# Linear attention with a rational feed-forward block on one core: scaling constants in three tasks, the last output products in another order, and a new instruction order

## The chip, the core and the metric

The kernel runs on one core of a Trainium2 chip. The metric is the device time of one execution in microseconds (us): of three runs before the change the median is 539.79 (539.32 to 540.35). The engines are TensorE (PE in the profile, its weight loads PEld), VectorE (DVE), ScalarE (ACT), GpSimd (POOL) and SyncE (SP), which issues all DMAs here.

## The reference

For each of 4 x 8 heads, a linear attention with decay runs over 768 steps of 48 values; its output, 3072 tokens of 384 values, goes through a feed-forward block whose function is a quotient of two polynomials:

```python
for t in range(S):
    kt, vt, rt = (k[:, :, t], v[:, :, t], r[:, :, t])
    cur = np.einsum('bhd,bhe->bhde', u[None] * kt, vt)
    y[:, :, t] = np.einsum('bhd,bhde->bhe', rt, state + cur)
    state = w[None, :, :, None] * state + np.einsum('bhd,bhe->bhde', kt, vt)
...
h = x @ w_in
P = a[0] + a[1] * h + a[2] * h2 + a[3] * h3
Q = 1.0 + np.abs(b[0]) * np.abs(h) + np.abs(b[1]) * h2
g = P / (Q + 1e-06)
return (g @ w_out).astype(np.float32)
```

w_in is 384 x 2048, w_out 2048 x 384; all is 32-bit float.

## The kernel before

*Attention.* Tokens are worked in 24 blocks of 128, two blocks a pair, 12 pairs. r and k are scaled by powers of the decay, which the start makes (wcol clamps the decays, cen is their power, pw and pk hold powers and inverses, wrn and wkn the same turned); each block is turned on TensorE (tr, tk, L517), and a pair then has products kv (L566), a (L545), and y in two parts (L595: from the state, then its own). VectorE evicts a through a mask (av, L553); vo is a copy of half of v at other partitions (made by att_v with a copy or a DMA), read by the second part of y. The bonus term is r times k (m, L498), times ub (L503), summed to dt (L508) and times v (L512). y is added to m (L611), and m is turned into x (L623), kept as a high part xth and a low part xtl (L637).

*Feed-forward.* 12 tiles of 256 tokens; the 2048 columns are cut in slots of 2 x 128 (the very last slot is cut in two of 128). Per slot: f1 makes h with three products per piece (high by high, low by high, high by low; L648), or, for the first tile, one with the full weights (L654). Ten instructions on ScalarE, VectorE and GpSimd make g of h: z, q, t, ln, exp on ScalarE (L701 to L721), u3, hi, p, d on VectorE (L725 to L741), lo mostly on GpSimd (L745). Then f2 adds to the output o, half a tile (hf) at a time, again three products per 128 columns (L658 to L660). When a tile's columns are all in, put_out evicts each half with the scale SG (L792 on ScalarE, L794 on VectorE, L787 where a partial sum is added), and put_dma sends it (L799).

*Weights* come as pieces of 32-bit words (sto of w_out, 384 KB; sti of w_in, 512 KB; L378), and are made into wfo and wfi (L401), a high part whio or whii (L424) and a low part wloo or wloi (L421).

*Constants of the slots' functions.* pro_beta (L263 to L274) takes absolute values of the coefficients on ScalarE, floors two of them on VectorE (ctmp, L268), takes ln and exp of half of it on ScalarE (root), and sets four constants on VectorE (L271 to L274), two of them in the PSUM tile in which ScalarE also writes (sqs). pro_squares (from L281) refines the root and makes the other constants. The q and t of every slot wait for it.

*Order.* Nothing is scheduled while the program is built: build() and prologue() list about 2200 tasks with their engines, dependencies and buffers, and the text ORDER names the tasks by number in the order in which placed() issues them, a letter choosing the engine (D, A, G) where there is a choice. "w3" stands for three fillers: products of zeros on TensorE (L980 into a tile of its own, L978 into an open output, to which they add nothing), 60 in all. Each engine works its own instructions in this order and waits by semaphores.

```python
        for n_, e in order:
            if n_ != "warm":
                fns[n_](ENG.get(e))
            elif began:
                nc.tensor.matmul(grown, wzero, wones, start=False, stop=False)
            else:
                nc.tensor.matmul(warm[:, 0:DM], wzero, wones, start=True, stop=True)
```

## Time and profile before

| | us |
|---|---|
| median of three runs (lowest, highest) | 539.79 (539.32, 540.35) |
| the profiled execution: its time | 540.16 |
| its span | 538.4 |
| busy in the span: TensorE | 518.8 (96%) |
| VectorE | 429.7 (80%) |
| ScalarE | 398.6 (74%) |
| GpSimd | 255.0 (47%) |

The profile is one execution; its times count from the start of the span. Its page gives busy times, the chain of work that ended last, and groups of instructions by line. The trace behind it answers questions on a stretch: the busy time of each engine in it, what an engine waited for, the instructions in order of time. L12 is line 12 of the kernel before; a duration is the busy time of an instruction, and "idle before <- X" is the time that its engine sat idle ahead of it and who ended that.

### The profile page before, as it was taken

The numbers are of one execution on the slowest core, as the hardware profiler recorded it, in microseconds if no ns is written. First come the engines' busy times: TensorE is split into PE (matmuls) and PEld (weight loads), VectorE is DVE, ScalarE is ACT, GpSimd is POOL, SyncE is SP. The second block draws the span as 40 slices with busy tenths as digits, with TensorE's granted clock in tenths as the row PEclk, the third lists the DMA queues.
The fourth block names the chain that finished last, engine by engine and source line by source line (L and its number), as shares of the span: only waits on it lengthen the run. The fifth ranks groups of instructions, "written<-read, shape, count | busy, mean of one in ns | idle before, by whom it ended". The sixth has DMA issues, their size and how long they took to land.

```text
span 538.4 us, 14858 instructions
## 1 busy us (share of the span) xinstructions
PE 518.8 (96%) x6111; PEld 492.5 (91%) x6111; DVE 429.7 (80%) x716; ACT 398.6 (74%) x648; POOL 255.0 (47%) x244
## 2 busy tenths in 40 slices
PE   7779999999999999999999999999999999999995
PEld 3558898899999999999999999999999999999994
DVE  5899998999889786786887787787886777686681
ACT  5889989997856669684787656777666767888791
POOL 2588981644554655635255444256444422233231
PEclk9999999999999999999999999999999999999998
DMA  8977454830004304023250023140030000000001
GB/s 177 281 180 184 129 128 138 177 68 1 1 17 89 84 19 72 1 61 66 40 118 1 2 61 80 33 86 6 16 75 2 15 18 1 2 29 1 31 1 35
DMA packets 91661, 34.07 MB, mean 63 GB/s; under 512 B 84929, under 2 KB 88002, under 8 KB 91586
## 3 DMA queue, kind: packets, MB, share of 16 engines
q1 hardware_dynamic: 91586, 33.05, 26.7%
q8 instruction: 50, 0.82, 0.6%
q14 instruction: 25, 0.20, 0.1%
HBM read 28.32 MB, written 4.72 MB: 61 GB/s over the span
## 4 chain that ended last, share of the span: by engine, by line
PE 84%; DVE 8%; ACT 3%; DMA 2%; issue 1%; SPq 0%; DVEq 0%; ACTq 0%
PE h L648 33%; PE o L658 12%; PE o L659 12%; PE o L660 12%; PE y L595 5%; PE a L545 2%; PE kv L566 2%; PE h L654 2%; DMA sto<-in_moe_w_out_dram 2%; PE tr L517 2%; PE tk L517 1%; PE x L623 1%; DVE q L735 1%; DVE g L731 1%; DVE pk L322 1%
## 5 line engine op out<-in xcount | busy, mean ns | idle before, releaser
L745 POOL TENSOR_TENSOR g<-q,z 128x512 fp32r<-128x512 f32 (+1 forms) x97 | 125.7, 1295 | 214.9 <-DVE q L741 126.7
L648 PE MATMUL h<-xth,whii 128*128 128x256 f32 x528 | 152.0, 288 | 2.0 <-DVE q L735 1.7
L648 PE MATMUL h<-xtl,whii 128*128 128x256 f32 x528 | 148.1, 280 | 0.0
L648 PE MATMUL h<-xth,wloi 128*128 128x256 f32 x528 | 148.0, 280 | 0.0
L658 PE MATMUL o<-whio,g 128*128 128x384 f32 x384 | 134.3, 350 | 0.0
L660 PE MATMUL o<-whio,g 128*128 128x384 f32 x384 | 130.0, 339 | 0.0
L659 PE MATMUL o<-wloo,g 128*128 128x384 f32 x384 | 130.0, 338 | 0.0
L648 PEld LDWEIGHTS h<-xth,whii 128*128 128x128 f32 x528 | 99.4, 188 | 4.5 <-DVE q L735 2.7
L648 PEld LDWEIGHTS h<-xtl,whii 128*128 128x128 f32 x528 | 99.5, 188 | 0.0
L648 PEld LDWEIGHTS h<-xth,wloi 128*128 128x128 f32 x528 | 99.5, 188 | 0.0
L707 ACT ACTIVATE w<-q,off,root 128x512 f32<-128x512 f32 (+1 forms) x97 | 75.3, 779 | 29.9 <-DVE q L735 15.9
L731 DVE SCALAR_TENSOR_TENSOR g<-h,sig,z 128x512 fp32r<-128x512 f32 (+1 forms) x97 | 72.0, 742 | 30.2 <-ACT z L721 26.5
L712 ACT ACTIVATE t<-h,off,root 128x512 f32<-128x512 f32 (+1 forms) x97 | 73.4, 767 | 24.1 <-PE h L648 21.6
L701 ACT ACTIVATE q<-h 128x512 f32<-128x512 f32 (+1 forms) x97 | 56.3, 587 | 37.6 <-PE h L648 36.0
L725 DVE SCALAR_TENSOR_TENSOR h<-t,sig,h 128x512 f32<-128x512 f32 (+1 forms) x97 | 71.7, 742 | 15.5 <-ACT t L712 12.3
L735 DVE SCALAR_TENSOR_TENSOR q<-w,sig,g 128x512 f32<-128x512 f32 (+1 forms) x97 | 72.1, 743 | 6.5
L741 DVE SCALAR_TENSOR_TENSOR q<-h,sig,q 128x512 f32<-128x512 f32 (+1 forms) x97 | 72.1, 744 | 2.7
L658 PEld LDWEIGHTS o<-whio,g 128*128 128x128 f32 x384 | 72.1, 188 | 1.1
L660 PEld LDWEIGHTS o<-whio,g 128*128 128x128 f32 x384 | 72.1, 188 | 0.5 <-POOL g L745 0.5
L659 PEld LDWEIGHTS o<-wloo,g 128*128 128x128 f32 x384 | 72.2, 188 | 0.0
L717 ACT ACTIVATE z<-w,lnb 128x512 f32<-128x512 f32 (+1 forms) x97 | 65.9, 679 | 8.4 <-POOL g L745 3.4
L721 ACT ACTIVATE z<-z,lnb 128x512 f32<-128x512 f32 (+1 forms) x97 | 69.7, 718 | 2.1
(144 smaller groups left out, 669.5 us busy)
## 6 DMA issues: line engine op xcount, KB each, us to landing
sto<-in_moe_w_out_dram SPq DMA_DIRECT2D x16, 384.0 KB, 4.0
sti<-in_moe_w_in_dram SPq DMA_DIRECT2D x12, 512.0 KB, 5.0
rh<-in_r_dram SPq DMA_DIRECT2D x24, 192.0 KB, 4.0
kh<-in_k_dram SPq DMA_DIRECT2D x24, 192.0 KB, 3.8
vn<-in_v_dram SPq DMA_DIRECT2D x24, 192.0 KB, 4.1
out_dram<-os SPq DMA_DIRECT2D x24, 192.0 KB, 2.6
vo<-in_v_dram SPq DMA_DIRECT2D x16, 96.0 KB, 3.8
wraw<-in_w_dram SPq DMA_DIRECT2D x1, 1.0 KB, 2.6
```

Source lines behind the costliest of these rows:

```text
L648: nc.tensor.matmul(o, w_[nm][:, c], x_[:, cc], start=(n == 0), stop=(n == 3 * NCC - 1))
L658: nc.tensor.matmul(o, hi, w_["hi"], start=first, stop=False)
L659: nc.tensor.matmul(o, hi, w_["lo"], start=False, stop=False)
L660: nc.tensor.matmul(o, lo, w_["hi"], start=False, stop=last)
L707: nc.scalar.activation(g["w"], w_, AF.Square, scale=RB, bias=KB)
L712: nc.scalar.activation(g["t"], g["h"], AF.Square, scale=RA, bias=KA)
L721: nc.scalar.activation(g["z"], g["z"], AF.Exp, scale=-1.0, bias=lnb[:, 1:2])
L725: nc.vector.scalar_tensor_tensor(g["h"], g["t"], KAP, g["h"], op0=ALU.add, op1=ALU.mult)
L731: nc.vector.scalar_tensor_tensor(g["hi"], g["h"], c0, g["z"], op0=ALU.add, op1=ALU.mult)
L735: nc.vector.scalar_tensor_tensor(g["q"], g.get("w", g["q"]), qe, g["hi"].bitcast(F32), op0=ALU.add, op1=ALU.mult)
L741: nc.vector.scalar_tensor_tensor(g["d"], g["h"], c0, g["q"], op0=ALU.add, op1=ALU.subtract)
L745: e.tensor_mul(g["lo"], g["d"], g["z"])
```

## The change

*Constants.* pro_beta becomes three tasks, which ORDER can place apart: the absolute values (ScalarE), the floor (VectorE), ln and exp (ScalarE). The four constants are set in pro_load, at the start; two of them get a tile of their own, pts, and pro_squares reads them there.

*The last output products.* The last two slots hold one piece of 128 columns each, with two half tiles hf: before, their f2 ran in the order (first slot, half 0), (first, 1), (last, 0), (last, 1); now (first, 0), (last, 0), (first, 1), (last, 1). The last eviction, of half 1, is cut in two of 192 columns: put_out does one on ScalarE, the new task put_rest the other on VectorE, and the DMA waits for the second.

*Order.* ORDER is a new text, with other places, engines and fillers (66) for the whole program.

```diff
 ORDER = """
-0 58 59 35 12 13 14 16 15 w1 60 61 62 17 18 20 234 156 157 w1 3 51 52 1 7 w15 243 w1 22 23 w3 10 233 236G 241 25 19 158 159 53
...
+236 158 247 0 1 60 6 37 14 3 7 4 w1 15 16 17 18 20 22 19 w16 29 159 160 161 162 163A 21 23 38 61 62 63 235 238G w2 12 13 248
...
+        tab["sq"] = ps_o.tile([P, 512], F32, tag="o0", name="sqs")
+        tab["pts"] = cst.tile([P, 2], F32, name="pts")
+        nc.vector.memset(tab["pts"][:, 0:1], 0.5)
+        nc.vector.memset(tab["pts"][:, 1:2], 1.0)
+        nc.vector.memset(lnb[:, 0:1], QC * 2.0 ** -LN_SHIFT)
+        nc.vector.memset(lnb[:, 1:2], -LN_SHIFT * math.log(2.0))
...
     def pro_beta():
         nc.scalar.activation(beta[:, 0:2], coef[:, 4:6], AF.Abs)
         nc.scalar.activation(cabs, coef, AF.Abs)
-        tab["sq"] = ps_o.tile([P, 512], F32, tag="o0", name="sqs")
-        half, pts = tab["sq"][:, 0:2], tab["sq"][:, 4:6]
+
+    def pro_floor():
         nc.vector.tensor_scalar(rx, cabs[:, 3:6:2], SMALL, None, op0=ALU.max)
+
+    def pro_root():
+        half = tab["sq"][:, 0:2]
         nc.scalar.activation(half, rx, AF.Ln)
         nc.scalar.activation(root, half, AF.Exp, scale=0.5)
-        nc.vector.memset(pts[:, 0:1], 0.5)
-        nc.vector.memset(pts[:, 1:2], 1.0)
-        nc.vector.memset(lnb[:, 0:1], QC * 2.0 ** -LN_SHIFT)
-        nc.vector.memset(lnb[:, 1:2], -LN_SHIFT * math.log(2.0))
...
-        half, raw, pts = (tab["sq"][:, x : x + 2] for x in (0, 2, 4))
+        half, raw, pts = tab["sq"][:, 0:2], tab["sq"][:, 2:4], tab["pts"]
...
+    EH = DM // 2
...
-        if e is nc.scalar:
+        if s == NS - 1 and hf:
+            nc.scalar.activation(os_[:, 0:EH], o_[:, 0:EH], AF.Copy, scale=SG)
+        elif e is nc.scalar:
             e.activation(os_, o_, AF.Copy, scale=SG)
...
+    def put_rest():
+        nc.vector.tensor_scalar(oss[NTILE - 1, 1][:, EH:DM], ops[NTILE - 1][1][:, EH:DM], SG, None, op0=ALU.mult)
...
+                if s >= NS - 2 and s + hf != NS - 2:
+                    prev = {(NS - 1, 0): ("f2", NS - 2, 0), (NS - 2, 1): ("f2", NS - 1, 0), (NS - 1, 1): ("f2", NS - 2, 1)}[s, hf]
...
+                    if end:
+                        add(("or",), lambda e: put_rest(), "D", [("os", s, hf)], use=[("o", so), buf])
...
-        add(("sq",), lambda e: pro_squares(), "D", [("beta",)])
+        add(("floor",), lambda e: pro_floor(), "D", [("beta",)])
+        add(("root",), lambda e: pro_root(), "A", [("floor",)])
+        add(("sq",), lambda e: pro_squares(), "D", [("root",)])
```

What stands where now, engine by engine. (Numbers at the end of a name tell buffers apart; the lines of the new kernel lie 5 to 12 further down.) First SyncE's issues at the start of the program, before and now:

```order
L236 DMA wraw<-in_w_dram 64x4x1
L237 DMA wraw<-in_w_dram 48x4x1
L378 DMA sto_129<-in_moe_w_out_dram 128x768
L467 DMA rh_101<-in_r_dram 128x8x48
L378 DMA sto_152<-in_moe_w_out_dram 128x768
L378 DMA sti_2_159<-in_moe_w_in_dram 128x1024
L261 DMA ur<-in_u_dram 1x384
L467 DMA kh_102<-in_k_dram 128x8x48
```

```order
L472 DMA rh_101<-in_r_dram 128x8x48
L383 DMA sto_117<-in_moe_w_out_dram 128x768
L472 DMA kh_104<-in_k_dram 128x8x48
L236 DMA wraw<-in_w_dram 64x4x1
L237 DMA wraw<-in_w_dram 48x4x1
L267 DMA ur<-in_u_dram 1x384
L383 DMA sto_141<-in_moe_w_out_dram 128x768
L472 DMA kh_102<-in_k_dram 128x8x48
L472 DMA rh_103<-in_r_dram 128x8x48
```

wraw (the decays) and ur stood first and seventh; now r, a piece of w_out and a k stand ahead of wraw.

Next VectorE's queue around the floor (ctmp), before and now:

```order
L424 CAST whii_2_230<-wfi_2_215 128x512
L490 TENSOR_TENSOR kh_102<-kh_102,wkn 128x8x48
L268 TENSOR_SCALAR ctmp<-cabs 128x2
L271 MEMSET sqs 128x1
L272 MEMSET sqs 128x1
L273 MEMSET lnb 128x1
L274 MEMSET lnb 128x1
L523 TENSOR_TENSOR kt<-tk_197,pk 112x512
L523 TENSOR_TENSOR kt<-tk_236,pk 112x512
```

```order
L406 SCALAR_TENSOR_TENSOR wfi_1_385<-cp_380,upi_1_382 128x512
L616 TENSOR_TENSOR m_200<-y_0_348,m_200 128x4x48
L616 TENSOR_TENSOR m_208<-y_0_348,m_208 128x4x48
L274 TENSOR_SCALAR ctmp<-cabs 128x2
L616 TENSOR_TENSOR m_200<-y_1_349,m_200 128x4x48
L429 CAST whii_1_447<-wfi_1_385 128x512
L616 TENSOR_TENSOR m_208<-y_1_349,m_208 128x4x48
L429 COPY xth_450<-x_439 128x3x128
L406 SCALAR_TENSOR_TENSOR wfi_0_456<-cp_389,upi_0_391 128x512
L406 SCALAR_TENSOR_TENSOR wfi_0_466<-cp_445,upi_0_453 128x512
L286 RECIPROCAL sqs<-root 128x2
```

The floor moved from ahead of the turned k and r (kt, rt) to among the additions of y to m; its reader on VectorE, the first instruction of pro_squares (the reciprocal), follows some way behind it, and the memsets are gone from here.

Then VectorE's queue shortly ahead of the first second-tile products (L648), at the masks av of the second pair, before and now:

```order
L577 TENSOR_TENSOR st_110<-kv_1_612,st_110 112x384
L553 TENSOR_TENSOR av<-a_0_670,mask 128x512
L725 SCALAR_TENSOR_TENSOR h_491<-t_591,sig,h_491 128x512
L401 SCALAR_TENSOR_TENSOR wfo_761<-cp_660,upo_664 128x384
L553 TENSOR_TENSOR av<-a_1_671,mask 128x512
L731 SCALAR_TENSOR_TENSOR g_821<-h_491,sig,z_758 128x512
L735 SCALAR_TENSOR_TENSOR q_651<-w_653,sig,g_821 128x512
L611 TENSOR_TENSOR m_463<-y_0_726,m_463 128x4x48
L611 TENSOR_TENSOR m_550<-y_0_726,m_550 128x4x48
L611 TENSOR_TENSOR m_463<-y_1_727,m_463 128x4x48
L741 SCALAR_TENSOR_TENSOR q_651<-h_491,sig,q_651 128x512
```

```order
L406 SCALAR_TENSOR_TENSOR wfi_1_612<-cp_585,upi_1_591 128x512
L429 COPY kt<-tk_607 112x512
L429 CAST whii_1_619<-wfi_1_612 128x512
L429 COPY st_110<-kv_0_630 112x384
L730 SCALAR_TENSOR_TENSOR h_527<-t_615,sig,h_527 128x512
L582 TENSOR_TENSOR st_110<-kv_1_631,st_110 112x384
L558 TENSOR_TENSOR av<-a_0_673,mask 128x512
L406 SCALAR_TENSOR_TENSOR wfo_709<-cp_626,upo_665 128x384
L429 COPY vo_112<-vn_580 64x192
L429 COPY vo_112<-vn_587 64x192
L558 TENSOR_TENSOR av<-a_1_674,mask 128x512
L736 SCALAR_TENSOR_TENSOR g_814<-h_527,sig,z_715 128x512
```

Two copies of vo and a cast whii now stand among the functions of the second slot (u3 at L725, now L730; hi at L731, now L736); these copies and casts stood on ScalarE.

Last the end of the program, with the semaphores that each instruction waits for: the last evictions on ScalarE before, on VectorE now (ScalarE's half, L799, waits for PE_49 alone among the engines).

```order
L721 ACTIVATE z_7484<-z_7484,lnb 128x256 [waits Activation_49]
L717 ACTIVATE z_7491<-w_7440,lnb 128x256 [waits Pool_49]
L721 ACTIVATE z_7491<-z_7491,lnb 128x256 [waits Activation_49]
L792 ACTIVATE os_0_7509<-o_0_7259,sig 128x384 [waits DMAHW5_49,PE_49]
L792 ACTIVATE os_1_7514<-o_1_7260,sig 128x384 [waits DMAHW6_49,DMAHW4_49,PE_49]
```

```order
L736 SCALAR_TENSOR_TENSOR g_7512<-h_7426,sig,z_7508 128x256 [waits DVE_49,PE_49,Activation_49]
L740 SCALAR_TENSOR_TENSOR q_7485<-w_7504,sig,g_7512 128x256 [waits DVE_49,Pool_49]
L746 SCALAR_TENSOR_TENSOR q_7485<-h_7426,sig,q_7485 128x256 [waits DVE_49]
L803 TENSOR_SCALAR os_0_7523<-o_0_7283,sig 128x384 [waits DMAHW4_49,PE_49]
L807 TENSOR_SCALAR os_1_7530<-o_1_7284,sig 128x192 [waits DMAHW5_49,DMAHW2_49,Activation_49]
```

VectorE now evicts half 0 (L803), and its half of half 1 (L807) waits for Activation_49, ScalarE's semaphore, at the count that ScalarE's half (L799) brings it to. On SyncE the output DMA of an early tile, whose data have long been there, now stands between the last two output DMAs.

More of the change, by code (lines that the diff above doesn't have):

```diff
@@ new lines @@
+1092 1040D 1046 1048 1049 1050 1051 1026 1063 1052 1053 1054G 1028 1062 1064 1065 1066 211 212A 1075 1076 1077 1067 1068 1069
+213D 1070G 1041 393G 1042 1055 1057 1056 1058 1078 1080 1079 1081 1082 1083 1093 1095 1098 1084D 1094 1096 1097 1099 401 403
+1071 1072 1105 1106 1107 1109 234G 1085 1086 379 380G 402 404 1088 408 1123 1087 435G 438G 436G 1100 1101 409 415 410 414 1102
+1108 1110 1111 1112 1113 1114 1089 1124 1127 1125 411 412A 413 1126 1137 1138 1139 1128 1115 1130 416 417D 418 1103 1104 420
@@ new lines @@
+1312 1344 1346 1347 510 511A 512 1349 1350 1358 1360 1361 1325 1326 1339 1340 1351 562 560 515 541 540A 561 563G 622 534G 565G
+566D 1359 1362 573 546 547 525A 539A 542 1369 1370 1363 544 1364 543 545 1352 1353 549 520 1365 521D 551 1371 1372 1374 1375
+1373 1376 556 1377 1378 1379 1387 1388 1389 1390 1391 1394 1366 1354 1367 1392 575 574 576G 577D 579D 1393 550 1401 1402 1403
+571 572A 1405 1395 1396 1397 1415 1416 1368 564G 569 1380 1381 1404 1406 1407 570A 578D 584 585A 1408 1409 1410 1398 1411 1412
@@ L127 @@
+2104 2105 2106 2107 2108 2112 2115 2125 2113 2114 2116 2080 2126 2139 2117 2081D 2082 2079 2140 2118 2127 2128 2130 2129 2095
[3 rows of a table added]
+2199 2201 2202 2203 2204 2205 2193 2206D 2207 1090 2208 2209 2210 2211
 """
@@ L931, in build @@
                     prv = [("os", max(s_ for s_ in range(s) if SL[s_][0] == f and closes(s_)), hf)] if some else []
-                    add(("os", s, hf), lambda e, s=s, hf=hf: put_out(s, hf, e), "D" if some else "AD", [("f2", s, hf), *prv],
+                    end = s == NS - 1 and hf == 1
+                    add(("os", s, hf), lambda e, s=s, hf=hf: put_out(s, hf, e), "A" if end else "D" if some else "AD", [("f2", s, hf), *prv],
                         new=[] if some else [(spare(s), buf)], use=[("o", so)] + ([buf] if some else []))
+                    if end:
+                        add(("or",), lambda e: put_rest(), "D", [("os", s, hf)], use=[("o", so), buf])
                     if done:
-                        add(("od", f, hf), lambda e, f=f, hf=hf: put_dma(f, hf), "S", [("os", s, hf)], use=[buf] + keep * (s == NS - 1))
+                        add(("od", f, hf), lambda e, f=f, hf=hf: put_dma(f, hf), "S", [("or",) if end else ("os", s, hf)], use=[buf] + keep * (s == NS - 1))
     def prologue():
```

139 lines of the change are left out of this document (65 added, 74 removed), and 13 rows, old and new, of the table ORDER.

## The prediction

> **What bounds the kernel now.** I read the page, then the busy time in three stretches, the fillers, the waits and the end. The first row is the page's busy time; the stretches give for each engine its busy time and count, then TensorE's granted clock, the DMA share and GB/s.
>
> ```profile
> PE 518.8 (96%) x6111; PEld 492.5 (91%) x6111; DVE 429.7 (80%) x716; ACT 398.6 (74%) x648; POOL 255.0 (47%) x244
> core 0: us, PE busy (x) PEld busy (x) DVE busy (x) ACT busy (x) POOL busy (x), PEclk, DMA share, GB/s
> 0.00:52.40 52.40, 41.57 (x674) 30.00 (x674) 42.67 (x94) 41.43 (x82) 33.41 (x47) 1.00 0.86 204
> 52.40:60.00 7.60, 7.36 (x174) 6.58 (x171) 7.35 (x14) 7.13 (x13) 5.48 (x6) 1.00 0.83 223
> 60.00:532.00 472.00, 469.91 (x5272) 455.91 (x5271) 379.71 (x610) 349.79 (x554) 216.12 (x191) 1.00 0.20 45
> L980 PE MATMUL warm<-wones,wzero 128*128 128x384 bf16 x45 | 12.2, 402 | 2.3 <-POOL wzero L245 2.3
> L978 PE MATMUL o<-wones,wzero 128*128 128x384 bf16 x10 | 2.5, 327 | 0.0
> 52.40 0.38 PE L648 MATMUL h<-xth,whii 128*128 128x256 f32 x1
> ```
>
> TensorE (PE) bounds the kernel from 52.40 us, where the first h product by two-part weights (L648) starts. From 60 us on it is busy 469.91 of 472.00, and 0.30 of the rest lies behind its last product (the eviction that waits for it starts at 531.70, below). So between 52.40 and the tail only 0.24 + 1.79 = 2.0 us are idle. Before 52.40 it is busy for 41.57 of 52.40, and 55 of the 60 fillers (products with zeros) stand there too. At the granted clock 1.00 everywhere, the time is therefore: when the first L648 product starts, plus a nearly solid stream of products, plus the tail. The products are the same before and after; what stands ahead of the first L648 product is the same set as well (three kv, two a and y groups, 12 products of L654, 12 of L658 to L660). So the change can win only the idle time of the start, the 2.0 us, or the tail.
>
> In the start VectorE (DVE) sets the pace: 42.67 busy of 52.40, idle mainly before its first result and in the waits of the next rows (time waited, how often, the longest). The last rows are what it does just before 52.40.
>
> ```profile
> DVE pw L315 <- ACT cen L309: 2.8, 1, 2.8
> DVE av L553 <- PE y L595: 1.0, 2, 0.8
> DVE av L553 <- PE a L545: 0.9, 1, 0.9
> 51.38 0.56 DVE L637 TENSOR_TENSOR xtl<-x,xth 128x384 fp32r<-128x384 f32 x1
> 51.85 0.68 DVE L424 COPY kt<-tk 112x512 f32<-112x512 f32 x1
> ```
>
> The product at 52.40 needs the second low half of x (L637), which ends at 51.94. Rows that follow each other without waiting start 0.08 sooner than the last one ends (51.38 + 0.56 against 51.85).
>
> The tail: end of the chain, the last evictions and output DMAs, the time from issue to landing of each of the two (the last row of each DMA answer), and the two slices of 1 us before the last landing.
>
> ```profile
> 531.70 0.58 ACT os L792
> 531.78 0.87 SPq L799 DMA_DIRECT2D out_dram<-os  x2
> out_dram<-os SPq DMA_DIRECT2D x1, 192.0 KB, 1.9
> out_dram<-os SPq DMA_DIRECT2D x1, 192.0 KB, 4.1
> 534.00:535.00 1.00, 0.00 (x0) 0.00 (x0) 0.00 (x0) 0.00 (x0) 0.00 (x0) 0.50 0.04 9
> 535.00:536.00 1.00, 0.00 (x0) 0.00 (x0) 0.00 (x0) 0.00 (x0) 0.00 (x0) 0.50 0.06 12
> q8 instruction: 50, 0.82, 0.6%
> ```
>
> The two DMAs of equal size start some 0.5 apart, yet one lands after 1.9 and the other after 4.1. In between, at 9 and 12 GB/s, only stragglers move. q8 carries instructions in pieces of 0.82 MB / 50 = 16 KB.
>
> **The change part by part.** (1) *Constants.* ScalarE (ACT) computes |b| and |a,b|, VectorE floors (ctmp), ScalarE takes ln and exp, VectorE sets constants. Before, all of it is one task:
>
> ```profile
> 14.86 1.07 DVE L268 TENSOR_SCALAR ctmp<-cabs 128x2 f32<-128x2 f32 x1
> 14.39 1.42 POOL L490 TENSOR_TENSOR kh<-kh,wkn 128x384 f32<-128x384 f32 x1 [0.28 <-ACT beta L264]
> 15.96 0.18 ACT L269 ACTIVATE sqs<-ctmp 128x2 f32<-128x2 f32 x1 [1.47 <-DVE ctmp L268]
> 16.41 0.06 DVE L271 MEMSET sqs<- 128x1 f32 x1 [0.48 <-ACT root L270]
> ```
>
> The floor, of 128x2, takes 1.07 and ends 0.12 after GpSimd's (POOL) kh product, at 15.81; then VectorE idles 0.48 for the root, since its memsets write the tile in which ScalarE works. From 14.86 to the first memset, at 16.41, 1.55 pass for a floor that alone takes about as long as wcol's 0.17 (next fence). Now the four memsets (0.06 each) stand at the program's start, where VectorE waits 2.68 for wcol, and other instructions stand between the floor and its reader. Gain on VectorE 1.55 - 0.17 + 0.1 for the memsets: -1.5; bounds -0.6 (the floor again waits 0.9 for GpSimd) and -1.6. ScalarE's 1.47 of waiting goes too; it isn't the pace here.
>
> (2) *Start.* The decays (wraw) are now issued behind the first r, a weight piece and the first k, not first. The next rows show a small transfer behind large ones, and ScalarE's first steps.
>
> ```profile
> 4.30 0.34 SPq L261 DMA_DIRECT2D ur<-in_u_dram  x1
> 9.88 0.91 PE L298 MATMUL us<-ur,ones 1*128 1x384 f32 x2 [0.56 <-DMA ur<-in_u_dram]
> 3.73 0.17 DVE L305 TENSOR_SCALAR wcol<-wraw 112x4 f32<-112x4 f32 x1 [2.68 <-DMA wraw<-in_w_dram]
> 5.75 0.52 ACT L396 ACTIVATE cp<-sto 128x384 f32<-128x384 f32 x1 [3.66 <-DMA sto<-in_moe_w_out_dram]
> 6.42 0.20 ACT L309 ACTIVATE cen<-sq 112x4 f32<-112x4 f32 x1
> ```
>
> ur, 1.5 KB issued at 4.30, is there at 9.88, 5.6 later: a small transfer lands behind the large ones issued before it. Ahead of wraw now stand 192 + 384 + 192 KB, 0.79 MB, which at the first stretch's 204 GB/s take 3.9. So wraw is there between 3.73 and 7.6; I take 6.4, nearer to the late end as ur is. Before, cen stands on ScalarE behind the weight piece (5.75) and ends at 6.62; now it is first there, and ends three steps of 0.2 behind wraw, at 7.1. Cost +0.5; bounds -2.3 and +1.6.
>
> (3) *Work moved to VectorE.* In its queue up to the second L637 (rows 3 to 91 before, 7 to 96 after) the new order has more: one PSUM copy of 512 (0.68, the row at 51.85), two casts whii (0.41 unhindered), one whio (0.35), two products of SBUF tiles (as L498, 0.55: by ub, and v by dt), four copies of vo (0.25). It has less: one wfo (0.54), one kh scaling (as L498) and two xth (0.55 each). The rows (min/median/max ns for three, then mean):
>
> ```profile
> L424 DVE COPY vo<-vn x4: 254/804/1375, 229.3 to 361.9; 64x192 f32<-64x192 f32 x4
> L424 DVE CAST whio<-wfo x11: 348/350/1419, 30.7 to 103.3; 128x384 fp32r<-128x384 f32 x11
> L424 DVE CAST whii<-wfi x6: 414/416/1366, 14.1 to 101.7; 128x512 fp32r<-128x512 f32 x6
> L424 DVE CAST whio<-wfo 128x384 fp32r<-128x384 f32 x11 | 6.7, 624 | 0.1
> L401 DVE SCALAR_TENSOR_TENSOR wfo<-cp,upo 128x384 int32<-128x384 int32 x15 | 8.2, 544 | 0.3 <-ACT upo L387 0.2
> L498 DVE TENSOR_TENSOR m<-rh,kh 128x384 f32<-128x384 f32 x1 | 0.6, 552 | 0.0
> L424 DVE CAST xth<-x 128x384 fp32r<-128x384 f32 x4 | 2.2, 546 | 0.0
> ```
>
> More: 0.68 + 0.82 + 0.35 + 1.10 + 1.00 = 3.95; less: 0.54 + 0.55 + 1.10 = 2.19; that is 1.76, and for six more instructions 6 x 0.08 of overlap off: +1.3.
>
> (4) *Waits for GpSimd.* Seven of these (whii, whio, vo) read and write SBUF only, and such instructions wait:
>
> ```profile
> 34.45 2.50 POOL L421 TENSOR_TENSOR wloi<-wfi,whii 128x512 fp32r<-128x512 f32 x2
> 35.83 1.34 DVE L424 CAST whio<-wfo 128x384 fp32r<-128x384 f32 x1
> ```
>
> The cast of 35.83 takes 1.34 instead of 0.35 and ends 0.22 after GpSimd's second product (at 36.95). By the ends, seven such waits cost 0 to 7 x (1.42 - 0.35) = 7.5. I take the mean of the whio rows over their shortest, 0.62 - 0.35 = 0.27, as nearest (11 casts, in the first 110 us): +1.9. The vo rows would give more, 0.80 - 0.25 = 0.55.
>
> (5) *Taken up by waits.* VectorE waited 1.0 + 0.9 for products a and y (rows above), and whio, two vo and a whii now stand ahead of the first av. What makes VectorE later there only shortens these waits, as long as TensorE isn't later too: -1.6, bounds -1.9 and 0.
>
> (6) *The y products behind the first L648.* Before, 18 h products cover the wait for av:
>
> ```profile
> 57.64 2.38 PE h L648 x18
> 56.89 0.69 DVE L553 TENSOR_TENSOR av<-a,mask 128x512 f32<-128x512 f32 x1 [0.25 <-PE y L595]
> ```
>
> The second av ends at 57.58, and y may start at 60.02. In the new order four fillers stand there, and the 18 products come behind y. The two av now stand behind a whio, a whii and one more product than before, 0.35 + 0.41 + 0.55 = 1.3, against which four fillers of 2.5 / 10 = 0.25 stand: +0.3, bounds 0 and 2.4 (the cover gone altogether). On the other side VectorE has by then done conversions that it did later before, which can take back some of the 2.0 us of idle: -1.2, bounds -2.0 and 0.
>
> (7) *Fillers.* Six of 66 stand behind the first L648 product, where five of 60 did; the others lie in idle time. At 0.25 each: +0.2.
>
> (8) *Tail.* The last half tile's second eviction is cut in halves of 192. But VectorE's half waits for ScalarE's semaphore at the count of ScalarE's half, so they run one behind the other. A half I estimate at 0.4 on either engine, from 0.58 for 384 with a fixed part: 0.4 + 0.1 + 0.4 against 0.58, +0.3. The first half tile closes 6 products before the end, not 3, so its DMA leaves some 0.5 sooner; but the output DMA of an early tile, moved here, now stands between the two on SP. The last landing hung on stragglers, which may hide these 0.3 or add to them: +0.2, bounds -2.2 (landing after 1.9, as its neighbour) and +0.9.
>
> Sum: -1.5 + 0.5 + 1.3 + 1.9 - 1.6 + 0.3 - 1.2 + 0.2 + 0.2 = +0.1, on the profiled execution's 540.16 (span 538.4 and 1.8 around it), which gives 540.3. That execution lies 0.37 above the median of the three runs, 539.79; on the median it is **539.9**.
>
> **The rivals.** *Slower: GpSimd holds VectorE up.* Its place is VectorE's queue ahead of the second L637, and GpSimd is busy 33.41 of the first 52.40. If the seven wait as the vo rows do, 7 x 0.55 = 3.9, 2.0 more than in (4): 541.9. It decides from a mean wait of 0.41 on (0.14 x 7 = 1.0 more, past 540.87). Against it: half of the whio casts took 0.35. [...]
>
> *Faster: the order fits.* If the moved instructions find GpSimd idle, (4) is 0; and if av is ready behind the fillers, 0.3 goes too: 539.9 - 1.9 - 0.3 = 537.7. For it: the floor's stall is surely gone, and 1.9 of VectorE's waits were there to be filled.
>
> *Faster: the last DMA lands like its neighbour.* Then 4.1 - 1.9 = 2.2 go from the tail, and with the 0.2 of (8) 537.5. For it: its first half tile is out of the way sooner. Against: an instruction piece of 16 KB moves near it, and the branch at the program's end stays where it is, just behind the last issue. [...]
>
> *The split does nothing:* part of (8); were the halves side by side, it would be 0.5 less, within the forecast's own case.
>
> **How the numbers follow.** A measurement of this kernel can tell about 0.2% from no change, here 1.08 us: the same is 538.71 to 540.87. My forecast, that gain and loss cancel, has 0.36, with a range of its own of 538.7 to 540.9. Slower by the waits for GpSimd has 0.31. Faster has 0.33: 0.25 for the order that fits, 0.08 for the landing. So faster 0.33, same 0.36, slower 0.31. The range reaches to both sides' own values, with some 0.3 and 0.7 to spare for the unsure terms (2) and (6): **537.4 to 542.6**.
>
> **What would show it.** In the changed kernel's trace: wraw's reader (wcol) at about 6.5 and cen's end at 7.1 (2); the floor without a wait behind it on ScalarE (1); vo, whio and whii on VectorE longer than 0.25, 0.35 and 0.41 while GpSimd is busy (4); the first L648 product at 51 to 54, against 52.40; an idle stretch of up to 1 ahead of the y products behind it (6); VectorE's half of the last eviction behind ScalarE's, and the last landing 4 behind its issue (8). I am wrong if the first L648 product starts before 50.5 (the order fits), if the seven casts and copies cost over 3 in waits, or if the landing comes 2 after its issue.

## The result and the profile after

The changed kernel takes 546.9 us, the median of three runs (546.67 to 549.31), against 539.79 (539.32 to 540.35) before: a ratio of 1.0138, 95% interval 1.0114 to 1.0162. It is 7.1 slower, far above the forecast of 539.9 and outside its range. The profiled execution is the longest of the three, 549.31 with a span of 547.6, 9.2 above that of before; it shows the kinds of loss, some of them larger than in the median. Single executions differ at two places even where nothing was changed: the profiles that share the old start have the first h product at 52.40, 53.04 and 53.92, and from the last product to the end of the span the six with the old tail take 5.1 to 6.7.

Its stretches: up to the first h product by two-part weights (now L653, at 56.34), to the first own half of the third pair's y, to the end of the 18 h products that follow it, and the rest. Columns as before: length, busy time of each engine, granted clock, DMA share, GB/s.

```profile
core 0: us, PE busy (x) PEld busy (x) DVE busy (x) ACT busy (x) POOL busy (x), PEclk, DMA share, GB/s
0.00:56.34 56.34, 41.76 (x678) 30.30 (x679) 47.60 (x101) 39.06 (x79) 33.17 (x47) 0.97 0.79 184
56.34:61.85 5.51, 5.35 (x152) 4.58 (x151) 5.32 (x12) 4.88 (x9) 0.35 (x1) 1.00 1.02 229
61.85:70.67 8.82, 6.10 (x83) 5.89 (x84) 5.59 (x13) 3.14 (x6) 3.57 (x4) 0.63 0.27 75
70.67:540.60 469.93, 468.24 (x5208) 455.04 (x5206) 385.69 (x618) 356.22 (x568) 198.22 (x172) 1.00 0.20 43
```

TensorE's work ahead of the first L653 is what it was (41.76 busy, 41.57 before), but it is spread over 56.34, not 52.40: 3.9 more, nearly all of it waiting. (Two more profiles of this start, "loads later" and "the old order of h and y" below, have 57.53 and 57.40 here; about 4 more than the old start, then.) In the third stretch it is busy 6.10 of 8.82, at a clock of 0.63. From 70.67 on it is solid again.

The next rows are the chain of work that ended last, from 58.83 on (start, length, engine and line), and the same place in the chain of before.

```profile
58.83 1.16 PE a L550 x64
59.99 1.08 PE y L600 x64
61.08 0.02 issue
61.10 0.70 DVE av L558
61.80 0.04 issue
61.85 0.66 PE y L600 x27
62.51 2.72 issue
65.22 1.31 PE y L600 x37
66.53 4.14 PE h L653 x18
```

```profile
57.64 2.38 PE h L648 x18
60.02 1.08 PE y L595 x64
61.10 0.38 PE o L658
```

By 61.10 the old kernel had behind it both the 18 h products and the y; the new one has the same behind it at 70.67. That is 9.6 later, 3.9 from ahead of the first L653 and 5.6 from here. The last h or o product ends at 540.64 against 531.68, so 0.6 of it is won back, and the tail behind that is 7.0 against 6.7: the 9.2.

In the second stop, of 2.72, the mask av is long there, and the trace names no engine: "issue". The DMA queues in that place show what is missing (two windows, 54.5 to 62.6 and 62.6 to 63.8; instructions travel on q8):

```profile
q1 hardware_dynamic: 2889, 1.41, 81.8%
```

```profile
q8 instruction: 1, 0.02, 5.8%
```

The one piece of 16 KB starts at 62.63, just behind the loads that fill the window before, and lands at 63.74; TensorE goes on at 65.22. Behind it the clock is down, and the same 18 products take 4.14 instead of 2.38, the 37 y products 1.31 instead of about 0.63:

```profile
65.20:70.90 5.70, 5.68 (x57) 5.49 (x57) 4.29 (x10) 0.72 (x2) 0.93 (x2) 0.50 0.14 56
```

Ahead of the first L653, what TensorE waited for most (total, times, longest); then the group of vo's copies on VectorE, two of them, and GpSimd's rows beside these:

```profile
PE tr L522 <- DVE rh L499: 3.8, 1, 3.8
PE tabk L336 <- DVE pk L327: 2.8, 2, 1.7
PE kv L571 <- POOL kh L495: 1.4, 1, 1.4
```

```profile
L429 DVE COPY vo<-vn 64x192 f32<-64x192 f32 x4 | 3.3, 870 | 0.1
```

```profile
46.74 2.09 DVE L429 COPY vo<-vn 64x192 f32<-64x192 f32 x2
```

```profile
46.43 1.29 POOL L426 TENSOR_TENSOR wloi<-wfi,whii 128x512 fp32r<-128x512 f32 x1
47.68 1.03 POOL L499 TENSOR_TENSOR rh<-rh,wrn 128x384 f32<-128x384 f32 x1
```

Two copies that alone take 0.25 each take 2.09, and end with a GpSimd product; the four take 3.3. The longest stop is TensorE's for the scaled r (rh), which stands far back in VectorE's queue, at 36.31; in it the clock falls too (36.00 to 40.00 at 0.60).

A third engine counts as well. The pages' rows of the chain that ended last, before and now:

```profile
PE 84%; DVE 8%; ACT 3%; DMA 2%; issue 1%; SPq 0%; DVEq 0%; ACTq 0%
PE 83%; DVE 7%; ACT 5%; issue 2%; DMA 1%; SPq 0%; DVEq 0%; ACTq 0%
```

ScalarE's share grows from 3% to 5%: in the changed kernel the chain runs on ScalarE alone from 36.48 to 49.49, where in the old one it runs on VectorE and then on TensorE.

The tail: the split evictions and the last transfer (KB, us from issue to landing).

```profile
541.13 0.42 DVE L807 TENSOR_SCALAR os<-o,sig 128x192 f32<-128x192 f32 x1 [0.90 <-ACT os L799]
540.67 0.42 ACT L799 ACTIVATE os<-o,sig 128x192 f32<-128x192 f32 x1 [5.87 <-PE o L665]
out_dram<-os SPq DMA_DIRECT2D x1, 192.0 KB, 4.1
```

### The profile page after: what moved, and what is told of

The parts are those of the page before. It is cut to its first block, busy times and chain, and to the rows that moved or that the text cites. A ratio compares the mean times of both kernels' runs of the same rounds, so it can differ in the third digit from the quotient of the medians.

```text
span 547.6 us, 14844 instructions
## 1 busy us (share of the span) xinstructions
PE 521.5 (95%) x6117; PEld 495.8 (91%) x6117; DVE 444.6 (81%) x742; ACT 403.7 (74%) x661; POOL 235.3 (43%) x222
## 4 chain that ended last, share of the span: by engine, by line
PE 83%; DVE 7%; ACT 5%; issue 2%; DMA 1%; SPq 0%; DVEq 0%; ACTq 0%
PE h L653 33%; PE o L663 12%; PE o L665 12%; PE o L664 11%; PE y L600 5%; PE h L659 2%; PE a L550 2%; PE kv L571 2%; PE tr L522 2%; PE tk L522 2%; PE x L628 1%; DVE wfo L406 1%; ACT z L722 1%; ACT w L712 1%; DVE whii L429 1%
## 5 line engine op out<-in xcount | busy, mean ns | idle before, releaser
L750 POOL TENSOR_TENSOR g<-q,z 128x512 fp32r<-128x512 f32 (+1 forms) x93 | 121.1, 1304 | 237.1 <-DVE q L746 155.3
L653 PE MATMUL h<-xth,whii 128*128 128x256 f32 x528 | 152.6, 289 | 0.1
L653 PE MATMUL h<-xtl,whii 128*128 128x256 f32 x528 | 148.9, 282 | 0.0
L653 PE MATMUL h<-xth,wloi 128*128 128x256 f32 x528 | 148.8, 282 | 0.0
L653 PEld LDWEIGHTS h<-xth,whii 128*128 128x128 f32 x528 | 100.1, 190 | 1.7 <-PE tk L522 0.3
L653 PEld LDWEIGHTS h<-xth,wloi 128*128 128x128 f32 x528 | 100.4, 190 | 0.0
L653 PEld LDWEIGHTS h<-xtl,whii 128*128 128x128 f32 x528 | 100.3, 190 | 0.0
L736 DVE SCALAR_TENSOR_TENSOR g<-h,sig,z 128x512 fp32r<-128x512 f32 (+1 forms) x97 | 72.0, 743 | 34.4 <-ACT z L726 30.1
L730 DVE SCALAR_TENSOR_TENSOR h<-t,sig,h 128x512 f32<-128x512 f32 (+1 forms) x97 | 71.5, 742 | 8.1 <-ACT t L717 6.6
```

The lines of the kernel that those rows point to most:

```text
L653: nc.tensor.matmul(o, w_[nm][:, c], x_[:, cc], start=(n == 0), stop=(n == 3 * NCC - 1))
L730: nc.vector.scalar_tensor_tensor(g["h"], g["t"], KAP, g["h"], op0=ALU.add, op1=ALU.mult)
L736: nc.vector.scalar_tensor_tensor(g["hi"], g["h"], c0, g["z"], op0=ALU.add, op1=ALU.mult)
L750: e.tensor_mul(g["lo"], g["d"], g["z"])
```

## What follows the y products

**Theory: the missing piece.** The 64 small y products and their weights, 128 instructions, run in 1.1 us, and 128 more follow; the next piece of instructions, 16 KB on q8, comes behind the loads in flight (it starts at 62.63) and lands when TensorE has already stopped. **Rival:** the new order is late as a whole, and this stop only takes time that would be lost anyway.

*Loads later.* In the new order, a k and a v load are issued behind the y products instead of ahead of them (in ORDER, 372 and 434 stand for them and the k behind).

```diff
- 352S 372 228 114A ... 101G 434 137 840
+ 352S 228 114A ... 101G 137 372 434 840
```

> The changed kernel with two of the five transfers that it issues at 55 to 58 us (a k and a v, both needed much later) queued behind the next weight piece, which waits for its buffer. Account: TensorE stands still at 62.51 to 65.22 because its next 16 KB of instructions land only at 63.74, behind these transfers; with two of them gone the piece comes sooner, the stall is below 1 us, the clock stays at 1.00 from 64 to 71 us, and the time falls by 4 to 5, to 542 to 543. Rival (VectorE alone: its queue is late, and TensorE would wait for it anyway): the idle time moves to a wait for VectorE and the time stays within 1.5 us of 546.9.

Measured: 544.96 (544.61 to 545.6), ratio 1.0087 (1.0055 to 1.0119) to the kernel before, against 1.0138. In the four us from 60.00 on and in the next four, the clock is whole:

```profile
60.00:64.00 4.00, 3.63 (x159) 2.94 (x160) 3.81 (x9) 3.75 (x7) 0.48 (x1) 1.00 0.34 95
64.00:68.00 4.00, 3.79 (x59) 3.64 (x59) 3.50 (x9) 2.84 (x7) 2.82 (x3) 1.00 0.69 173
```

The stop is 0.52 instead of 2.72, and y and the 18 products are done at 67.31, 3.4 sooner, although the first L653 comes at 57.53, 1.2 later. No engine's work was changed: the stop is the fetch behind the loads. The other runs below bear it out: in the five profiles of the new order that leave these loads and y in place, the stop is 2.16 to 2.72 (the clock falls behind it in three of the five); in the four with the loads moved it is 0.26 to 0.81. By the ratios it is worth about 0.5%, 2.8 us, of the 1.4%.

Over the changed kernel's span q8 carries 0.82 MB in 50 pieces. Its list of TensorE's waits has two stops that are put down to "issue", 3.0 in all: 0.33 behind TensorE's record 449, in the first pair's y, and 2.72 behind its record 1729, here. So most of the pieces cost no stop that is listed; the long one stands among small products, with loads in flight.

*The old order of h and y.* In the new order, the 18 h products stand ahead of the y again.

```diff
- w2 361 367 ... 832G 835 836 851
+ w2 835 836 361 367 ... 832G 851
```

> The changed kernel with the 18 L653 products of the slot that follows y put ahead of y's own part, as the old order has it. They issue 36 instructions in 2.4 us where the small products issue 128 in 1.1, and give the instruction piece time to land. Account: no stall inside y, clock 1.00 from 60 to 75 us, time 541.5 to 543. Rival (VectorE alone): no more than 1.5 us gained.

Measured: 547.27 (546.66 to 548.2), ratio 1.0128 (1.0093 to 1.0162). The stop is 0.48 (the chain's "issue" at 65.59), and yet nothing is gained: y is 2.4 later, and VectorE and then TensorE wait for what comes of it.

```profile
67.18 0.62 DVE L616 TENSOR_TENSOR m<-y,m 128x192 f32<-128x192 f32 x2 [2.73 <-PE y L600]
```

```profile
PE h L659 <- DVE m L616: 1.7, 1, 1.7
```

So the order of the two can't be blamed by itself. That the new start, late as it is, needs y early, and that y early runs into the fetch, is how these rows read; no run shows it apart.

*The same move in the kernel before.* Its y group ahead of the 18 products (359 is the y).

```diff
- 105D w3 833 834 226 ... 825 827 359 361
+ 105D w3 359 833 834 226 ... 825 827 361
```

> The kernel before with the two groups exchanged: y's own part of the third pair directly ahead of the 18 L648 products, not behind them. Account: three groups of small products (kv apart) then follow each other and run through the instructions that have been fetched: a stall of 1.5 to 3 us inside or ahead of y, the clock at 0.5 for some 3 to 6 us after it, time 542 to 545. Rival (only the wait for av decides): idle up to 0.9 ahead of y, clock 1.00, time 539.8 to 540.8.

Measured: 542.91 (541.37 to 545.2, 10 runs), ratio 1.005 (1.003 to 1.0069). The stop comes with the move, in the middle of y:

```profile
58.27 0.86 PE y L595 x32
59.13 1.04 issue
60.17 0.68 PE y L595 x32
60.85 2.31 PE h L648 x18
```

It is 1.04 long, the piece lands at 58.65, and the clock stays at 1.00; x then waits 0.8 further on. The move alone makes the old kernel 2.7 slower.

## The two halves, and the constants

*Only the start old, only the start new.* The old order for the first 406 entries with the new one behind it; and the new order up to the first L653 with the old one behind it, and the new tail.

```diff
- ORDER: new entries, start to end
+ ORDER: old entries (renumbered) up to the 406th, then new
```

> The changed kernel's code, constants and tail with a mixed order: the old order for the first 406 entries (up to the second x of the sixth block, about 70 us), then the rest as the new order has it. Account: all that the change loses lies in the first 70 us (by work done, TensorE is 9.7 us later at 62 us of the kernel before, and only 9.0 later at the end), so the time is 538.5 to 540.3, and the clock stays at 1.00. Rival (the new order costs time all along, by fewer gaps to hide work in): 543 or more.

```diff
- ORDER: new entries, start to end
+ ORDER: new entries up to the first L653, then old (renumbered)
```

> The reverse: the new order up to the first L653 product, then the old order with its 18 products ahead of y's own part, and the new tail. Account: the new start costs about 4 and no more than that follows, since the stall inside y of the third pair is gone: 543 to 545. Rival (a late start is taken back by the idle time that follows): 541 or less. Rival (the stall is set by the start): 546 or more.

Measured: 547.61 (ratio 1.0145, 1.011 to 1.018) and 547.7 (1.0138, 1.0109 to 1.0168). Each loses all of it, but each also has a seam of its own, so they don't divide the loss. The first waits 1.98 at 80.66, with the clock down behind it; its first L653 comes at 56.83, although the order there is the old one. The second starts L653 at 60.56, and 3.1 of that is the seam: 19 fillers more stand right ahead of it. Its time is that of the third theory, but there is no stop in the third pair's y; without the seam's 3.1 it would be at 544.6, by this estimate, where the first theory had it. What the first half shows is that the old order with the new constants starts late; hence the next.

*Only the constants.* The kernel before, with the three tasks and the tile pts.

```diff
-246 2 8 255
+248 2 8 9 10 257
+        tab["pts"] = cst.tile([P, 2], F32, name="pts")
```

> The kernel before with the constants' change alone: three tasks, issued in the old place one behind the other, the four memsets at the start. My step (1): VectorE's stall of 0.48 for the root goes, the floor still waits for GpSimd: 0.3 to 0.6 less for VectorE, of which the waits for products a and y just behind it may take all: 539.2 to 540.0. Rival (step (1) in full): 538.3.

Measured: 543.89 (543.11 to 547.89), ratio 1.0088 (1.0054 to 1.0122). This part was forecast to gain 1.5. Two steps of pro_squares, one element wide, stand out on VectorE (L291 and L299); next to them GpSimd's rows:

```profile
30.07 2.67 DVE L291 SCALAR_TENSOR_TENSOR sig<-sig,pts 128x1 f32<-128x1 f32 x1
...
34.04 0.72 DVE L299 SCALAR_TENSOR_TENSOR lnb<-sig,pts 128x1 f32<-128x1 f32 x1
```

```profile
29.98 0.82 POOL L620 TENSOR_TENSOR st<-st,w 112x384 f32<-112x384 f32 x1
30.77 1.00 POOL L426 TENSOR_TENSOR wloo<-wfo,whio 128x384 fp32r<-128x384 f32 x1
31.73 0.99 POOL L503 TENSOR_TENSOR m<-rh,kh 128x384 f32<-128x384 f32 x1
```

L291 starts just behind GpSimd's st, at 30.07, and ends at 32.74, with GpSimd's m, at 32.72: it stood through three products. Before, the constants lay in sqs, a PSUM tile; pts lies in SBUF, and with it every operand of these steps.

*The constants in PSUM.* The same kernel, with pts in two spare columns of a PSUM tile.

```diff
-        tab["pts"] = cst.tile([P, 2], F32, name="pts")
+        tab["pts"] = tab["sq"][:, 4:6]
```

> The constants' change alone in the old order, but with the two constants pts kept in the PSUM tile, where the kernel before had them (still set at the start). Theory: with pts in SBUF four steps of pro_squares have all operands in SBUF, and one of them waited 2.5 for GpSimd, another 0.56; in PSUM they take 0.15 to 0.25 again, VectorE is some 3 earlier at its second low half of x, and the time is 539 to 540.5. Rival (the new places of the memsets or the missing wait for the root change what TensorE does at 8 to 20 us, where its clock fell): 542.5 to 544 as with pts in SBUF.

Measured: 540.54 (539.07 to 542.47, 11 runs), ratio 1.0008 (0.999 to 1.0026). The same two steps, while GpSimd is as busy (its wloo of 1.01 starts at 30.85):

```profile
30.27 0.16 DVE L291 SCALAR_TENSOR_TENSOR sig<-sig,sqs 128x1 f32<-128x1 f32 x1
...
31.77 0.15 DVE L299 SCALAR_TENSOR_TENSOR lnb<-sig,sqs 128x1 f32<-128x1 f32 x1
```

The two constants moved from SBUF to PSUM are worth 543.89 - 540.54 = 3.35 in the old order (0.8% by the ratios). At L291 the step takes 0.16 instead of 2.67 and at L299 0.15 instead of 0.72; the first of these waits ran over three of GpSimd's instructions.

*The floor as well.* A third Abs on ScalarE puts the floor's input into PSUM too, which should show the gain of term (1) by itself.

```diff
+        nc.scalar.activation(tab["sq"][:, 6:8], coef[:, 3:6:2], AF.Abs)
-        nc.vector.tensor_scalar(rx, cabs[:, 3:6:2], SMALL, None, op0=ALU.max)
+        nc.vector.tensor_scalar(rx, tab["sq"][:, 6:8], SMALL, None, op0=ALU.max)
```

> As the constants' change with pts in PSUM, and the floor reads its two coefficients from PSUM too (a third, small absolute value on ScalarE writes them there), so that it does not wait for GpSimd's kh product. Step (1) in full: VectorE 1.4 sooner at the turned k and r of the first pair, of which the waits behind it take most: 538.3 to 539.8. Rival: no change against pts in PSUM alone, within 0.4.

Measured: 540.1 (538.33 to 542.09), ratio 0.9994 (0.9974 to 1.0014). VectorE does win at 15 us (the scaled r, rt, starts at 16.02, and at 16.14 with pts alone in PSUM, against 17.74 before), but the 1.5 isn't there at the end: it waits for the product a just behind.

*The same in the new order.* The changed kernel with pts in PSUM.

```diff
-        tab["pts"] = cst.tile([P, 2], F32, name="pts")
+        tab["pts"] = tab["sq"][:, 4:6]
```

> The changed kernel with pts in the PSUM tile and nothing else. Its profile shows one wait of 0.84 at lnb and none at the other three steps, so the theory gives only 0.3 to 1 less than 546.9: 545.9 to 546.9. Rival (this is what the change loses in the start): 543.

Measured: 547.49 (546.87 to 547.77), ratio 1.0131 (1.0104 to 1.0157): nothing. In the new order only L299 waited, 1.00 instead of 0.15, so this trap explains nothing that shows of the changed kernel's loss, though it decides the part on its own.

## The start of the new order

*Copies of vo back on ScalarE.* Two tasks, four copies, from VectorE to ScalarE.

```diff
-260D ... 305D
+260A ... 305A
```

> The changed kernel with the four vo copies of the first two pairs that it gave to VectorE done on ScalarE (as before the change). Account: up to its first L653 product (56.34, before 52.40) the changed kernel is paced by VectorE, whose four copies took 3.5 us there instead of 1.0; the first L653 product then comes 2.5 to 3.3 us sooner, at 53.0 to 53.9, and the time falls to 543.5 to 544.5 as long as the stall of TensorE at 62.5 stays. Rival (the clock's first fall, at 36 to 40 us, sets the lateness): the first L653 product stays at 56 and the time within 1 us of 546.9.

Measured: 548.2 (547.37 to 549.19), ratio 1.014 (1.0105 to 1.0175). The waits in the vo rows are gone, the second low half of x ends at 55.96 (55.65 in the changed kernel), and the first L653 comes at 56.66. VectorE now stands for y: 1.8 where the first pair's y itself stops for 1.82, 1.12 ahead of an av and 0.70 ahead of an m. And the copies went to the engine on which the chain ran: it lies on ScalarE from 37.12 to 50.06 here, 13 us as in the changed kernel. A price read off VectorE's queue is not a price of the kernel.

*The decays first.* wraw is issued ahead of r, a weight piece and k.

```diff
-236 158 247 0 1 60
+0 236 158 247 1 60
```

> The changed kernel with the decays' two DMAs issued first again, ahead of the first r, weight piece and k. My step (2) priced their late place at +0.5: 546.2 to 546.6 if that is right. Rival (the late decays shift the whole attention of the first pair, and so the 4 us of the start): wcol at 3.7, kv of the first pair 1.5 to 2.5 sooner, 543.5 to 545.

Measured: 545.42 (543.7 to 548.91), ratio 1.0101 (1.0049 to 1.0153); the first L653 comes at 54.33, 2.0 sooner.

```profile
3.75 0.17 DVE L310 TENSOR_SCALAR wcol<-wraw 112x4 f32<-112x4 f32 x1 [2.65 <-DMA wraw<-in_w_dram]
4.42 0.17 DVE L320 COPY pw<-cen 112x4 f32<-112x4 f32 x1 [0.51 <-ACT cen L314]
```

pw starts at 4.42, not at 7.17 (6.66 in the old order); since cen now has no weight piece ahead of it, the new order could have had more than the old one had. The interval is wide, but in "the two that paid" below, which has this start too, the first L653 comes at 55.51, again sooner than in the three profiles of the new start.

*Other loads behind the first pair's y.* A k and an r are issued behind a weight piece instead of ahead of it.

```diff
-11 5 278 279 281G 282G 287 284G 67 68
+11 5 67 278 279 281G 282G 287 284G 68
```

> The changed kernel with the loads of the third block's k and r issued behind the next weight piece (which waits for its buffer until about 22) instead of ahead of it. Theory: the instruction piece that y of the first pair waits for then lands sooner: the stall at 22 to 25 us is below 0.5 and the clock stays at 1.00 from 25 to 33 us; 544.5 to 546. Rival (the loads of weights alone fill the DMA engines): stall and time as before, 546.5 to 548.

Measured: 550.81 (549.38 to 551.71), ratio 1.0188 (1.0155 to 1.022): slower still. The stop in the first pair's y is 0.60 (0.33 in the changed kernel's profile), and the wait for rh has grown, to 4.9:

```profile
PE tr L522 <- DVE rh L499: 4.9, 1, 4.9
```

Neither expectation held. The clock is at 0.50 from 36 to 42.7. That the late k and r make rh late is only argued.

*Fewer fillers.* The kernel before without the 15 fillers ahead of the first transposes.

```diff
-1 7 w15 243 w1
+1 7 243 w1
```

> The kernel before without the group of 15 fillers that TensorE works at 5 to 8 us. They lie in idle time, so without a clock that follows TensorE's activity nothing changes (540.3 within 0.5). If the clock falls after some 3 us of idle time, it is 0.5 for some 3 to 6 us after 8 us, and the products of the tables and the first pair are late: 541.5 to 544.

Measured: 540.45 (538.9 to 541.96), ratio 0.9994 (0.9974 to 1.0015). An idle stretch of 3.50 takes their place. The view has the clock of 7 to 11 us at 1.00, but four transposes take 1.07 there; the last row is four of them in the kernel before:

```profile
6.66 1.07 PE L517 MATMUL tr<-ident,rh 128*112 128x128 f32 x4 [3.50 <-DMA rh<-in_r_dram]
7.00:11.00 4.00, 3.44 (x12) 1.83 (x10) 4.00 (x8) 2.03 (x5) 0.00 (x0) 1.00 1.10 255
```

```profile
14.05 0.60 PE L517 MATMUL tr<-ident,rh 128*112 128x128 f32 x4
```

The trace holds no clock record ahead of 17.37 (8.00 in the profile of before), and a stretch without one is shown as 1.00. By the durations TensorE ran at a lower rate until then: the four transposes at 15.04 still take 1.06. Without these fillers the products of the tables and of the first pair were therefore slow for longer than expected, and it cost nothing that shows at the end. The first 8 us of the kernel before are such a stretch too: 17 fillers take 5.62 there, 0.33 each, where five at 36.25 take 0.98, 0.20 each.

## The tail

*The whole tail, and its order alone.* The kernel before with the regrouped products and the split eviction; and with the regrouping, but the last half tile evicted whole on ScalarE.

```diff
+ f2 in the order (first, 0), (last, 0), (first, 1), (last, 1)
+ add(("or",), lambda e: put_rest(), "D", [("os", s, hf)], ...)
```

> The kernel before with the regrouped last products and the split eviction alone. My step (8): the halves run one behind the other, +0.2 to +0.3, so 539.9 to 540.4, and the last DMA lands some 4 behind its issue. Rival (it lands after 2, as its neighbour): 537.6 to 538.

```diff
+ f2 in the order (first, 0), (last, 0), (first, 1), (last, 1)
+    def put_rest():
+        pass
```

> The kernel before with the last products regrouped, the last eviction whole on ScalarE and the first half tile's on VectorE. Step (8) without the split: the last eviction takes 0.58, not 0.9, so 0.3 less than the tail alone had: 539.9 to 541.0, no difference to the kernel before that can be told. Rival (the regrouping itself delays the last DMA): 541.5 or more.

Measured: 541.54 (539.82 to 542.92, 11 runs), ratio 1.002 (1.0003 to 1.0036), and 539.58 (538.32 to 542.27, 11 runs), ratio 0.9993 (0.9976 to 1.0009). The landing that was expected of the first is not shown. The regrouping costs nothing that shows; with the split, the tail costs 0.2 to 1.9 by its interval.

The regrouped kernel's profile teaches something else. Up to its last slots it issues what the kernel before issues, and yet its first L648 comes at 53.92, not 52.40, with the clock at 0.50 for 10.2 us ahead of that (for none in the profile of before), while its last DMA lands after 2.3, not 4.1: 540.04 against 540.16, by two differences that nobody made.

## Mends together

*Four mends in the new order.* The constants in PSUM, the loads later, vo on ScalarE, and some scalings of r and their loads earlier; then, besides, the decays first, the two loads by the first pair's y later, and a scaling of k on VectorE instead of GpSimd.

```diff
-81 82 83 84 85
+292 291 294G 81 82 83 84 296D 85
```

> The changed kernel with four things mended: pts in the PSUM tile, the k and v of later blocks loaded behind the next weight piece, the four vo copies of the first two pairs on ScalarE, and the scaling of the fourth block's r (and its loads) ahead of four conversions in VectorE's queue, so that TensorE does not wait 3.8 for it. Theory (these waits and the clock that falls behind them are the loss): the first L653 product at 53 to 55, no idle stretch over 2 from 25 us on, clock 1.00 from 35 us on, time 540 to 542.5. Rival (the waits only move to the next instruction of the same full queue): 544 or more.

```diff
-239G ... 67 278 279
+239D ... 278 279 67
```

> All four mends of after_mended, with the decays first, the first block's k scaled on VectorE (as in the old order) instead of GpSimd, and the third block's k and r loaded later. Theory (these are what the start is late by): the first L653 product at 52.5 to 54, no stall over 1 inside y, 539.5 to 542. Rival (the new order's start is slower as a whole): 544 or more.

Measured: 545.67 (544.96 to 546.05), ratio 1.0098 (1.0071 to 1.0124), and 543.72 (543.01 to 544.58), ratio 1.0057 (1.0038 to 1.0076). In the first, TensorE's wait for rh is gone, and a stop of 2.07 in the first pair's y has come, with the clock at 0.5 from 26 to 36; the first L653 is later, at 57.95. In the second that stop is 2.30, and one of 3.2 has come in front of the turned k:

```profile
PE tk L522 <- ACT rt L429: 3.2, 1, 3.2
PE y L600 <- issue: 3.1, 2, 2.3
```

*The two that paid.* The decays first and the loads later, nothing else.

```diff
-236 158 247 0 1 60 ... 352S 372 228 ... 434 137
+0 236 158 247 1 60 ... 352S 228 ... 137 372 434
```

> The changed kernel with the decays issued first and the k and v of later blocks loaded behind the next weight piece, nothing else. Theory (two separate losses): the gains add up, 2.0 and 1.9 off 546.9 or a little more: 542.5 to 543.8, with a stall below 1 inside y of the third pair. Rival (both move the same stall in time): 544.5 to 545.5, as each alone.

Measured: 543.52 (542.74 to 545.33), ratio 1.0074 (1.0053 to 1.0095). 1.0138 - 1.0074 is 0.64%, 3.5 of the 7.4 that the change costs by its ratio; the two alone gave 2.0 and 2.8. The stop in the third pair's y is 0.78, as expected. None of the versions beats the kernel before.

## Why the prediction was wrong

The working rested on one sentence, "At the granted clock 1.00 everywhere", and on TensorE's stream being solid behind the first L653. That failed, and step (6) with it. The sum of (1) to (5), +0.6 for the start, failed too: the first L653 is 3.9 later in the profile.

- **(6), y ahead of the h products: +0.3 expected, -1.2 beside it.** The 18 products were priced as a cover for the wait for av. av was in time (61.10 + 0.70, and y starts at 61.85), but the products also covered the fetch: with their weights they are 36 instructions in 2.38 (57.64 to 60.02 before), and a piece of 16 KB landed under them, at 58.08. In the new order the small instructions, 128 in 1.1, had run out at 62.51, and the piece, which came behind the loads, landed at 63.74. The stop and the clock behind it made 5.6 in the profiled execution, where the clock fell; by loads later, 2.8 in the median. None of the rivals held this. Its sign and its place were in no row of before: what could have been seen there is how many instructions stand between two groups, and q8's 16 KB.
- **(3) and (4), VectorE's extra work and its waits for GpSimd: +1.3 and +1.9.** The kind was right, the size wasn't. Up to the end of the second low half of x VectorE is busy for 46.91 of 55.65, against 42.21 of 51.94 before: 4.7 more. The four vo copies alone waited 2.3 (3.3 - 4 x 0.25) and four whii casts 0.8 (2.4 - 4 x 0.41), together just over the 3 that the prediction had named as a sign of being wrong; the whio casts waited some 0.6 less than before. "The mean of the whio rows", 0.27 each, had been taken; the vo rows, the nearer ones, would have given 3.9. But the price didn't carry over to the end: vo on ScalarE gained nothing.
- **(1), the constants: -1.5.** It failed by what it left out: pts made steps read SBUF only. In the old order that costs 3.35; in the new one 0.85 at one step, and nothing that shows at the end. The gain is there on VectorE in the old order (rt 1.6 to 1.7 sooner) and not at the end (constants with floor in PSUM: 0.9994): the wait for a behind it took it, so it had no place in the sum beside (5).
- **(2), the decays behind other loads: +0.5.** By itself right: wcol at 6.49, cen's end at 7.13 (6.5 and 7.1 expected; the rows of the changed kernel's VectorE and ScalarE follow). That another place would give 2.0 was missed, since the comparison was with the old start and not with what the new one could be. But the late decays are not why the new start is slower than the old, by these profiles: from the first pw to the first product it takes 49.2 (7.17 to 56.34), and 49.9 with the decays first (4.42 to 54.33), where the old one takes 45.7 (6.66 to 52.40).

```profile
6.49 0.17 DVE L310 TENSOR_SCALAR wcol<-wraw 112x4 f32<-112x4 f32 x1 [5.40 <-DMA wraw<-in_w_dram]
7.17 0.17 DVE L320 COPY pw<-cen 112x4 f32<-112x4 f32 x1 [0.51 <-ACT cen L314]
```

```profile
6.93 0.20 ACT L314 ACTIVATE cen<-sq 112x4 f32<-112x4 f32 x1
```

- **(5), taken up by waits: -1.6.** Right in kind: VectorE idles 8.74 of 55.65, not 9.73 of 51.94, 1.0 less.
- **(7), fillers,** cost little or nothing: to judge by the old start, where 15 fewer make 0.9994.
- **(8), the tail: +0.2.** The halves do run one behind the other (0.42 and 0.42, the second waiting for ScalarE). That the two profiles agree with +0.2 (7.0 behind the last product against 6.7) and that the landing takes 4.1 again is luck: with the old tail the stretch behind the last product is 5.1 to 6.7 in six profiles, with the new one 5.3 to 7.1 in the ten made from the new order. The run of the tail alone gives 0.2 to 1.9 for it, with the 0.2 at the lower end.

The rival on the slower side, "GpSimd holds VectorE up", had the mechanism of the vo rows and about their amount, 3.9, but not what limits the kernel: its 541.9 is 5.0 below the median.

By its terms the forecast put the first L653 at 53.0; it came at 56.34. By the ratios 4.0 of 7.4 are left with the two mends, and 3.1 with all of them: so much of the start is not settled. VectorE's work and waits, ScalarE's unbroken stretch from 36.48 to 49.49 and the stops in the first pair's y are left as candidates. The clock is hardly one of its own: the regrouped kernel has it at 0.50 for 10.2 us ahead of a first product at 53.92, the changed kernel for 3.4 us ahead of one at 56.34. The candidates take each other's place when one is mended, and the stop in the first pair's y was 0.33 in the changed kernel's profile and 2.88 with nothing but pts moved to PSUM, so one execution doesn't tell what mends it.

## What to carry to other kernels

When small products are moved next to each other, count the instructions and see which loads are in flight where the next 16 KB of them are fetched: the 18 long products (2.38) between two such groups were cover for the fetch here, not only for data, and with y ahead of them TensorE stood for 2.72 in the new order and for 1.04 in the old one. Whether a small operand lies in PSUM or in SBUF is a question of order: a step of one element that read SBUF only stood through three of GpSimd's products, 2.67 instead of 0.16 (constants only). And where TensorE sets the pace, an idle stretch is priced with the clock that may fall behind it, not by its length alone: behind the stop of 2.72 the 18 products took 4.14 instead of 2.38. In the start, where TensorE waits anyway, some 10 us at a lower rate (four transposes in 1.07 instead of 0.60) cost nothing that showed: fewer fillers, ratio 0.9994.

## What the runs showed of the hardware

- *Fetch.* TensorE resumed 1.3 to 1.5 us after its piece of 16 KB had landed (63.74 and 65.22; 58.65 and 60.17 in the old kernel with y first; 62.91 and 64.22 with the loads later). The piece started at 62.63 in the changed kernel, when the loads were through, and already at 61.83 with two of them moved, although TensorE was later there.
- *Clock.* In the changed kernel it fell from 1.00 to 0.50 at 64.10, 1.6 into a stop of 2.72, and was back at 70.93, 5.7 after work resumed; in the wait for rh it fell 3.6 after the idle began and was back 3.2 after work resumed. It didn't fall in an idle stretch of 3.20 (decays first), nor behind the stop of 2.44 in y there. The stretches at 0.50 in the starts of these traces last 3.4, 6.8 or 10.2.
- *VectorE beside GpSimd.* A 128x1 step of VectorE took 2.67 with pts in SBUF, over three GpSimd products, and 0.16 with pts in PSUM; two copies that read one SBUF tile and write another (vo in the changed kernel) took 2.09, and ended with a GpSimd product, where each alone takes 0.25.
- *The last landing.* The same 192 KB at the end of the program took 2.5 to 4.2 from issue to landing in the six profiles with the old tail.
